# Windowed attention and a gated unit on one core: each transfer waits until few others stand in front of it in the queue, and the planner models instruction fetches

## The chip, the cores and the metric

The kernel runs on one core of one Trainium2 chip. Its five engines work side by side: PE (TensorE, matmuls and transposes), DVE (VectorE), ACT (ScalarE), POOL (GpSimd) and SP (SyncE, which here only issues transfers). Sixteen DMA engines move the data between HBM and the core's SBUF. The metric is the time of one execution on the device in microseconds; the median of three runs before the change is 193.21 us (190.97 to 197.29).

## The reference

Two stages follow each other. The first is attention over a window, for 8 batches of 8 heads with 576 positions of 64 elements; heads 0 to 3 see the last 32 positions ("plain"), heads 4 to 7 every fourth of the last 128 ("dilated"):

```python
mask_plain = (rel >= 0) & (rel < window)
mask_dil = (rel >= 0) & (rel < window * dilation) & (rel % dilation == 0)
attn = softmax(where(mask, q @ k.T / 8, -1e9))        # 8 x 8 x 576 x 576
x = (attn @ v).transpose(0, 2, 1, 3).reshape(8, 576, 512)
```

The second is a gated unit on x, a causal convolution of five taps for the gate and two dense layers:

```python
gate = sigmoid(sum(conv_w[k] * xp[:, k:k + S, :] for k in range(5)))   # xp: x, 4 zero rows ahead
out = (gate * (x @ w_val)) @ w_out                                     # 8 x 576 x 512
```

Inputs and output are float32; the kernel computes in bfloat16 with float32 sums.

## The kernel before

The attention is cut into 16 units: one for the four dilated and one for the four plain heads of each batch (`units`). The first of a batch is the dilated one, except in the last batch. Each unit is worked on in these steps:

- SP loads q and k (`load_q`, 576 KB each) and v (`load_vd` in two pieces of 320 and 448 KB, `load_vp` in two of 384 KB). There are three buffers for q and for k (`qns`, `kns`) and two for each v.
- POOL, or another engine, casts v to bfloat16, and q and k too for a plain unit (`cvq`, `cvk`, `cvv`, `cvp`).
- PE transposes q and k (`transposes`, L431); ACT and DVE copy the result out of PSUM.
- PE makes the scores in four parts (`scores`, L450), ACT takes their exponential (L470), DVE multiplies by the mask (L476), PE multiplies with v (`attn_d` L487, `attn_p` L514), and DVE divides by the sum.
- PE transposes the result (L535, L551), and ACT or DVE copies it to `xT`, where x stands with its channels on partitions.

After both units of a batch, PE runs the convolution (`conv`, L569), ACT a tanh, PE the dense layer with `w_val` (`val`, L584) and DVE the gate; then, over tiles of 128 rows, PE the layer with `w_out` (`outs`, L600), ACT copies the result to one of six tiles `osb` (L605), and SP stores it (`store`, L614). The weights are loaded in halves of 512 KB into `wst` (`load_w`) and cast. Where PE would have nothing to do at the start, it runs matmuls on a tile `warm` (L627), which nobody reads.

The order of all this is not written out. A planner in the kernel (`Plan`) lists every step as a `Task` with an estimated time on each engine that can do it, its dependences and a key; `KEY` holds an offset for each kind of step. At build time `run` goes through the tasks in the order of a modelled clock: `start_of` tells when a task could start, `commit` books it, and among those that could start soon the lowest key wins. The tasks are then emitted in the order of their modelled starts. On the chip each engine works through its own list in order and waits by semaphores for what it needs. The modelled times have no further effect.

Three parts of the planner matter here. A transfer is modelled to occupy the DMA for `load` after a fixed delay (`commit`); no more than eight transfers may be under way (`LANES`, in `start_of`); and all loads are chained in one order (`lane`). On the chip nothing but the eight semaphores of the transfers, used in turn, and the buffers hold SP back.

SP's list holds loads and stores in one order, so a store that waits for its copy holds the loads behind it.

Of the kernel before, what the change touches and what calls it, by code (L numbers as in the profile page):

```python
# [13 lines left out]
def hi_bf16(ap: bass.AP) -> bass.AP:  # L14
# [5 lines left out]
KEY = {"L": 107.8, "cv": -124.6, "T": -1.8, "ET": -73.4, "S": -44.5, "X": -131.1, "M": -134.6, "A": -61.1,  # L20
       "N": -69.6, "XT": -4.5, "XE": -25.9, "C": -13.0, "H": -17.0, "V": 4.2, "G": -107.0, "O":
       16.7, "P": -80.5, "SP": 2, "W": 23.7, "WV": 0, "WO": 1}


class Task:


    def __init__(self, name, key, opts, emit, deps=(), cfg=None, need=None,
                 frees=(), load=0.0, port=(), after=None):
        self.name, self.key, self.opts, self.emit = name, key, opts, emit  # L30
        self.deps = [d for d in deps if d is not None]
        self.cfg, self.need, self.load, self.port = cfg, need, load, port
        self.frees = [f for f in frees if f is not None]
        self.after = after
        self.holders = 0
        for f in self.frees:
            f.holders += 1
        self.fin = None
        self.slot = None


class Plan:
# [3 lines left out]
    LANES = 8  # L46
    SWITCH = 0.095
# [5 lines left out]
    def __init__(self, pairs, score_pairs):  # L53
        self.tasks = []
        self.free_at = {e: 0.0 for e in self.SLACK}
        self.banks = [0.0] * (2 * pairs)
        self.score_pairs = score_pairs
        self.scores = []
        self.cfg = None
        self.dma = 0.0  # L60
        self.lanes = []
        self.port = {"DVE": 0.0, "POOL": 0.0}
        self.idle = None
        self.done = []
# [22 lines left out]
    def start_of(self, t, eng):  # L87
        s = self.free_at[eng]
        if eng == "PE" and t.cfg != self.cfg and self.cfg is not None:
            s += self.SWITCH  # L90
        for d in t.deps:
            s = max(s, d.fin + self.LAT)
        if t.after:
            s = max(s, t.after.start)
        if eng in t.port:
            s = max(s, self.port["POOL" if eng == "DVE" else "DVE"])
        s = max(s, self.slot_for(t)[0])
        if t.load:

            while True:  # L100
                n = sum(1 for a, _ in self.lanes if a <= s)
                if n < self.LANES or self.lanes[n - self.LANES][1] <= s:
                    break
                s = self.lanes[n - self.LANES][1]
        return s
# [7 lines left out]
    def commit(self, t, eng, s):  # L113
        inf = float("inf")
        occ, lat = t.opts[eng]
        before = self.free_at[eng]
        self.free_at[eng] = s + occ
        t.fin = s + lat
        if t.load:
            self.dma = max(self.dma, s + 1.4) + t.load  # L120
            t.fin = self.dma + 0.6
            self.lanes = sorted(self.lanes + [(s, t.fin)])
        if eng in t.port:
            self.port[eng] = s + lat
        if eng == "PE":
            self.cfg = t.cfg
            self.fill(before, s)
        if t.need:
            t.slot = self.slot_for(t)[1]
            for n in t.slot:  # L130
                self.banks[n] = inf
            if t.need == "score":
                self.scores.append(inf)
                t.order = len(self.scores) - 1
            t.last = 0.0
        for f in t.frees:
            f.holders -= 1
            f.last = max(f.last, t.fin + self.LAT)
            if f.holders == 0:
                for n in f.slot:  # L140
                    self.banks[n] = f.last
                if f.need == "score":
                    self.scores[f.order] = f.last
        t.start, t.eng = s, eng
        self.done.append(t)
# [13 lines left out]
    def run(self):  # L159
        todo = list(self.tasks)  # L160
        waiting = {}
        users = {}
        ready = []
        for t in todo:
            deps = t.deps + ([t.after] if t.after else [])
            waiting[t] = len(deps)
            for d in deps:
                users.setdefault(d, []).append(t)
            if not deps:
                ready.append(t)  # L170
        inf = float("inf")
        while ready:
            best = None
            for eng in self.free_at:
                c = [(self.start_of(t, eng), t.key, t) for t in ready
                     if eng in t.opts and self.fits(t, eng)]
                c = [x for x in c if x[0] < inf]
                if not c:
                    continue
                s0 = min(x[0] for x in c)  # L180
                s, k, t = min((x for x in c if x[0] <= s0 + self.SLACK[eng]), key=lambda x: (
                    x[1] + (KEY["W"] if eng == "PE" and x[2].cfg != self.cfg else 0.0), x[0]))
                if best is None or (s, k) < best[:2]:
                    best = (s, k, t, eng)
            s, _, t, eng = best
            ready.remove(t)
            self.commit(t, eng, s)
            for n in users.get(t, []):
                waiting[n] -= 1
                if not waiting[n]:  # L190
                    ready.append(n)
        assert all(t.fin is not None for t in todo)
        for t in sorted(self.done, key=lambda t: t.start):
            t.emit(t)
# [3 lines left out]
def kernel(  # L198
# [10 lines left out]
    nc = tc.nc  # L209
# [5 lines left out]
    R = 4  # L215
# [158 lines left out]
    def dma(name, key, load, emit, deps=(), eng="SP", lane=None):  # L374
        t = plan.add(name, key, {eng: (0.45, 0.45)}, lambda t: emit(), deps, load=load,
                     after=lane and lane[0])
        if lane:
            lane[0] = t
        return t

    d_cw = dma("conv_nat", -60, 0.05,
               lambda: nc.scalar.dma_start(out=conv_nat, in_=moe_conv_w), eng="ACT")

    def load_q(u, name):
# [4 lines left out]
        if d:  # L389
            nc.sync.dma_start(  # L390
                out=dst, in_=src[b, hs].rearrange("h (p j) d -> (h p) (j d)", j=JD))
        else:
            nc.sync.dma_start(
                out=dst.rearrange("p (x f) -> p x f", x=2),
                in_=src[b, hs].rearrange("(x e) (p j) d -> (e p) x (j d)", x=2, j=JP))

    def load_vd(u, n, z):
        b = units[u][0]
        rows = v[b, 4:8].rearrange("h (p r) d -> p h (r d)", r=R)
        if z == 0:  # L400
            nc.sync.dma_start(out=vas[z][n % 2], in_=rows[0:KB[0]])
        else:
            nc.sync.dma_start(out=vas[z][n % 2][Z1:KB[1]], in_=rows[T1 + Z1:TT])

    def load_vp(u, n, half):
# [3 lines left out]
        skip = 1 if b == 0 and half == 0 else 0  # L409
        if skip:  # L410
            nc.sync.dma_start(
                out=vps[n % 2][W // 2:64, 0].rearrange("p s d -> p (s d)"),
                in_=bass.AP(tensor=v.tensor, offset=v.offset,
                            ap=[[2 * D, 64 - W // 2], [1, 2 * D]]))
        nc.sync.dma_start(
            out=dst[:, skip:].rearrange("p n s d -> p n (s d)"),
            in_=bass.AP(tensor=v.tensor, offset=first + skip * 192 * D,
                        ap=[[2 * D, 64], [192 * D, 4 * NG - skip], [1, 2 * D]]))
# [190 lines left out]
    def store(f, n, z):  # L609
        o = 0  # L610
        while o < 128:
            b, c = (128 * n + o) // HALF, (128 * n + o) % HALF
            ln = min(128 - o, HALF - c)
            nc.sync.dma_start(out=out[b, f * HALF + c:f * HALF + c + ln, :],  # L614
                              in_=osb[z % NO][o:o + ln])
            o += ln

# [24 lines left out]
    def load_w(name, src, dst, key):  # L642
        parts = []
        for half in range(2):
            deps = [W_OK["val"][2 * half], W_OK["val"][2 * half + 1]] if name == "out" else []
            ld = dma(f"w_{name}{half}", key, 1.6, lambda half=half: nc.sync.dma_start(
                out=wst[half],
                in_=src.rearrange("(c p) n -> p c n", p=128)[:, 2 * half:2 * half + 2]), deps, lane=lane)
# [38 lines left out]
    for u in range(NU):  # L687
# [4 lines left out]
        for name, L, TQ in (("q", ldq, Tq), ("k", ldk, Tk)):  # L692
# [7 lines left out]
            L[u] = dma(f"ld{name}{u}", j0 + KEY["L"], 1.75 if d else 1.85, lambda u=u, name=name: load_q(u, name), dep, lane=lane)  # L700
        if d:
            dep = [cvv[(same[-2], e, z)] for e in range(2) for z in range(2)] if len(same) > 1 else []
            ldv[u] = [dma(f"vd{z}{u}", j0 + KEY["L"], (1.25, 1.75)[z],
# [3 lines left out]
        else:  # L707
            dep = [cvp[2 * same[-2] + e] for e in range(2)] if len(same) > 1 else [c_dv]
            ldv[u] = [dma(f"vp{u}{h}", j0 + KEY["L"], 2.0,
# [18 lines left out]
        for name, L, C, TQ, EV in (("q", ldq, cvq, Tq, Eq), ("k", ldk, cvk, Tk, Ek)):  # L728
            TQ[u] = add(f"T{name}{u}", j0 + KEY["T"], {"PE": (0.50, 0.67)},
                        lambda t, u=u, name=name: transposes(t, u, name),  # L730
                        [L[u] if d else C[u], c_eye], cfg="F", need="pair")
# [4 lines left out]
        for e in range(2):  # L736
# [29 lines left out]
            for h in range(2):  # L766
# [3 lines left out]
                                 cfg="R" if d else "Q", need="score")  # L770
# [11 lines left out]
                if d:  # L782
# [3 lines left out]
                                     cfg="F", frees=[SC[(i, h)]])  # L786
# [6 lines left out]
                elif h == 1:  # L793
                    a = add(f"A{i}", j + KEY["A"], {"PE": (0.39, 0.56)},
                            lambda t, sc=SC[(i, 1)], i=i: attn_p(t, sc, i),
                            [MA[(i, 0)], MA[(i, 1)], cvp[i]], cfg="R", frees=[SC[(i, 1)]])
# [9 lines left out]
            if d:  # L806
                XT[i] = add(f"XT{i}", jx + KEY["XT"], {"PE": (0.27, 0.44)},
                            lambda t, i=i: transpose_xd(t, i),
                            [NM[(i, 0)], NM[(i, 1)]], cfg="F", need="bank")
# [3 lines left out]
            elif e == 1:  # L813
                XT[(u,)] = add(f"XT{i}", jx + KEY["XT"], {"PE": (0.52, 0.69)},
                               lambda t, u=u: transpose_xp(t, u),
                               [NM[(i, 1)], NM[(i - 1, 1)]], cfg="F", need="pair")
# [7 lines left out]
        for n, c in enumerate((2, 3, 0, 1)):  # L824
            CV[(b, c)] = add(f"C{b}{c}", j1 + KEY["C"] + n, {"PE": (0.60, 0.77)},
                             lambda t, b=b, c=c: conv(t, b, c),
                             [XE[(b, c)], T_DG], cfg="Q", need="pair")
# [3 lines left out]
        for n, c in enumerate((2, 3, 0, 1)):  # L831
# [3 lines left out]
                             cfg="F", need="pair")  # L835
# [6 lines left out]
    for n in range(NF):  # L842
        for f in range(2):
# [5 lines left out]
                     + (W_OX if f else W_OK["out"]), cfg="F", need="bank")  # L849
# [3 lines left out]
            ST.append(dma(f"st{f}{n}", key - 20, 0.8, lambda f=f, n=n, z=z: store(f, n, z), [cp]))  # L853
# [32 lines left out]
```

## Time and profile before

| what | value |
|---|---|
| median of three runs | 193.21 us |
| the profiled execution: its own time, span in the profile | 193.35 us, 191.4 us |
| PE busy; of it the filler matmuls (L627) | 166.2 us; 15.7 us |
| DVE, ACT, POOL busy | 128.4, 123.0, 61.7 us |
| moved by DMA | 43.41 MB, mean 227 GB/s |
| issue to landing, median: q, k, vp | 9.8, 11.3, 11.4 us |
| issue to landing, median: a store of 256 KB | 2.6 us |
| granted TensorE clock | 0.988 |

In the profile a line such as `L584` is a line of the kernel before. The page gives each engine's busy time, then the span in 40 slices of 4.8 us with a digit for the busy share of each, the DMA queues, the chain of work that ended last, and the groups of instructions. In the chain in order of time, a line has its start, its length and what the chain went through there; "issue" is time in which an engine waited for nothing that the profile shows. A line of waits has the waiting engine, what it waited for, the total in us, how often, and the longest. A line of DMA issues has the count, the size of each and the median time from issue to landing.

### The profile page before, as it was taken

How to read it: one execution, taken by the hardware profiler on the slowest of the kernel's cores; microseconds unless marked ns; L12 is line 12 of the kernel's file. 1: busy time of each engine (PE TensorE's matmuls, PEld its weight loads, DVE VectorE, ACT ScalarE, POOL GpSimd, SP SyncE). 2: the span in 40 equal slices, each digit the busy share in tenths (PEclk: the TensorE clock that was granted, in tenths of full speed). 3: DMA queues.
4: the chain of work that ended last, by engine and by line, in shares of the span. 5: the costliest groups of instructions: out<-in, count | busy, mean ns of one | idle time of the engine just before them, and what ended most of it. 6: DMA issues, size and time to landing. Idle time of an engine off the chain costs nothing.

```text
span 191.4 us, 6733 instructions
## 1 busy us (share of the span) xinstructions
PE 166.2 (87%) x2892; PEld 113.2 (59%) x2892; DVE 128.4 (67%) x239; ACT 123.0 (64%) x204; POOL 61.7 (32%) x99
## 2 busy tenths in 40 slices
PE   7999988788888779989896998989999989999890
PEld 2546456655676547766673765655675876757540
DVE  7498585967576858667877576997667978930500
ACT  2448976575796839768845577775786394658151
POOL 7964308236332552803632207351007000000000
PEclk9999999999999999999999699999999999999998
DMA  5999999999999999999999839996451312035256
GB/s 199 269 384 235 379 255 288 234 264 278 232 341 335 252 290 233 366 294 303 296 210 269 245 115 259 361 246 247 169 172 52 113 58 110 3 104 160 68 169 215
DMA packets 32102, 43.41 MB, mean 227 GB/s; under 512 B 1877, under 2 KB 20293, under 8 KB 32074
## 3 DMA queue, kind: packets, MB, share of 16 engines
q1 hardware_dynamic: 32064, 42.99, 81.3%
q8 instruction: 22, 0.36, 0.9%
q14 instruction: 6, 0.05, 0.1%
q10 hardware_dynamic: 10, 0.01, 0.1%
HBM read 33.56 MB, written 9.44 MB: 225 GB/s over the span
## 4 chain that ended last, share of the span: by engine, by line
PE 57%; DVE 12%; ACT 11%; DMA 9%; issue 6%; POOL 1%; ACTq 0%; SPq 0%; DVEq 0%
PE ps L600 14%; PE ps L584 13%; DMA kn<-in_k_dram 8%; PE ps L569 7%; PE ps L627 6%; PE ps L431 5%; PE ps L450 4%; ACT et L470 4%; PE ps L487 3%; ACT osb L605 3%; DVE et L476 3%; PE ps L514 2%; PE ps L535 2%; DVE qT L294 2%; ACT qT L292 2%
## 5 line engine op out<-in xcount | busy, mean ns | idle before, releaser
L470 ACT ACTIVATE et<-ps 128x576 bf16<-128x576 f32 x64 | 40.6, 653 | 17.4 <-PE ps L450 17.2
L584 PE MATMUL ps<-xT,w_val 128*128 128x288 bf16 x256 | 36.0, 286 | 3.5 <-issue 2.2
L600 PE MATMUL ps<-w_out,gy 128*128 128x512 bf16 x144 | 35.7, 380 | 2.9 <-ACT osb L605 1.9
L593 DVE SCALAR_TENSOR_TENSOR gy<-gy,ps 128x576 bf16<-128x576 bf16 x32 | 23.9, 750 | 14.9 <-PE ps L584 14.7
L605 ACT ACTIVATE osb<-ps 128x512 f32<-128x512 f32 x35 | 20.0, 598 | 18.9 <-PE ps L600 17.0
L294 POOL CAST vd<-va 80x512 bf16<-80x512 f32 (+1 forms) x32 | 20.7, 678 | 33.1 <-DMA va<-in_v_dram 14.2
L584 PEld LDWEIGHTS <-w_val 128*128 128x128 bf16 x256 | 23.7, 98 | 11.2 <-issue 5.6
L569 PE MATMUL ps<-xT,diag 64*64 64x288 bf16 x640 | 25.1, 287 | 2.4 <-issue 0.7
L294 POOL CAST vpb<-vp 128x768 bf16<-128x768 f32 x16 | 13.5, 863 | 38.6 <-DMA vp<-in_v_dram 21.7
L476 DVE TENSOR_TENSOR et<-et,mask_p 128x576 bf16<-128x576 bf16 x32 | 18.7, 591 | 7.0 <-ACT et L470 6.3
L476 DVE TENSOR_TENSOR et<-et,mask_d 128x576 bf16<-128x576 bf16 x32 | 20.2, 636 | 4.3 <-ACT et L470 3.9
L497 DVE TENSOR_TENSOR xnd<-ps,rec 72x512 bf16<-72x512 f32 x32 | 22.0, 687 | 1.1
L600 PEld LDWEIGHTS <-gy 128*128 128x128 bf16 x144 | 12.7, 98 | 15.6 <-issue 3.1
L577 ACT ACTIVATE gy<-ps 128x576 bf16<-128x576 f32 x32 | 20.2, 658 | 2.7 <-PE ps L569 2.5
L569 PEld LDWEIGHTS <-diag 64*64 64x64 bf16 x640 | 18.0, 107 | 5.3 <-issue 3.4
L292 ACT COPY xT<-ps 128x576 bf16<-128x576 bf16 (+1 forms) x20 | 15.7, 786 | 7.2 <-PE ps L551 3.7
L292 ACT COPY qT<-ps 128x576 bf16<-128x576 bf16 x22 | 13.6, 643 | 10.5 <-PE ps L431 7.8
L450 PE MATMUL ps<-qT,kT 64*64 64x96 bf16 (+1 forms) x640 | 18.6, 203 | 1.6 <-ACT kT L292 1.0
L450 PEld LDWEIGHTS <-kT 64*64 64x64 bf16 (+1 forms) x640 | 12.4, 102 | 12.3 <-issue 8.1
L627 PE MATMUL ps<-warm 128*128 128x512 bf16 x52 | 15.7, 429 | 1.3 <-DVE warm L314 1.3
L292 ACT COPY kT<-ps 128x576 bf16<-128x576 bf16 x21 | 12.9, 644 | 4.6 <-PE ps L431 2.7
L526 DVE TENSOR_TENSOR xnp<-ps,den 96x768 bf16<-96x768 f32 x16 | 15.3, 954 | 0.5
(68 smaller groups left out, 181.1 us busy)
## 6 DMA issues: line engine op xcount, KB each, us to landing
qn<-in_q_dram SPq DMA_DIRECT2D x16, 576.0 KB, 9.8
kn<-in_k_dram SPq DMA_DIRECT2D x16, 576.0 KB, 11.3
out_dram<-osb SPq DMA_DIRECT2D x24, 256.0 KB, 2.6
vp<-in_v_dram SPq DMA_DIRECT2D x15, 384.0 KB, 11.4
va<-in_v_dram SPq DMA_DIRECT2D x8, 448.0 KB, 9.9
va<-in_v_dram SPq DMA_DIRECT2D x8, 320.0 KB, 7.1
out_dram<-osb SPq DMA_DIRECT2D x8, 192.0 KB, 2.4
wst<-in_moe_w_val_dram SPq DMA_DIRECT2D x2, 512.0 KB, 8.4
```

The costliest lines, as they stand in the source:

```text
L292: nc.scalar.copy(out=dst, in_=src)
L294: op(t.eng).tensor_copy(dst, src)
L450: nc.tensor.matmul(out=ps[po:po + pn, x, out_c:out_c + ln], lhsT=kw[rb, k0:k0 + (pn - 1) * kstep + 1:kstep], rhs=qT[rb, q0:q0 + (ln - 1) * ...
L470: nc.scalar.activation(out=ets[(2 * i + hf) % NE][:, :, 0:HALF], in_=ps[:, :, 0:HALF], func=AF.Exp, scale=scale)
L476: op(t.eng).tensor_tensor(out=ev, in0=ev, in1=m.to_broadcast([128, 2, HALF]), op=ALU.mult)
L497: nc.vector.tensor_tensor(out=xnd[i % 2][:, 4 * hf:4 * hf + 4].rearrange("p (x j) h d -> p x (j h) d", x=2), in0=av[:, :, :, 0:D], in1=rec ...
L569: nc.tensor.matmul(out=ps[o:o + 64, 512 * f:512 * f + HALF], lhsT=diag[lo:lo + 64, c * K + kk, :], rhs=xT[lo:lo + 64, b % NX, c, f * HALF ...
L584: nc.tensor.matmul(out=ps[:, 512 * f:512 * f + HALF], lhsT=w_val[f][:, mc, c * 128:(c + 1) * 128], rhs=xT[:, b % NX, mc, K - 1 + f * HALF: ...
L593: nc.vector.scalar_tensor_tensor(out=y, in0=y, scalar=1.0, in1=ps[:, :, 0:HALF], op0=ALU.add, op1=ALU.mult)
L600: nc.tensor.matmul(out=ps, lhsT=y[:, c, 128 * n:128 * n + 128], rhs=w_out[f][:, c, :], start=(c == 0), stop=(c == NCH - 1))
L605: nc.scalar.activation(out=osb[z % NO], in_=bank(ou), func=AF.Copy, scale=0.5)
L627: plan.idle = lambda t: nc.tensor.matmul(out=bank(t), lhsT=warm[:, 0:128], rhs=warm, start=True, stop=True)
```

## The change

Three things change together.

Each transfer that SP issues is made to wait for an earlier one. The planner keeps the list of SP's transfers with their modelled starts (`queue`). `last_out` walks back from a transfer and adds up the `load` of those in front of it; the first at which the sum exceeds `QUEUED` (2.5 us) is the one that has to have landed. `start_of` uses it in the model, and when the kernel is emitted the same transfer is added as a dependence on the chip (`go` in `dma`). To that end the functions that load and store return their instructions.

The planner models the fetching of PE's program: tasks carry their number of matmuls (`mm`); after every `LINE` (125) matmuls a fetch of `FETCH` (1.3 us) is booked on the modelled DMA, and PE cannot pass into a block before its fetch is over.

The constants of the model and all of `KEY` are new: `load` is 1.5 us for q and k instead of 1.75 and 1.85, 1.2 and 1.6 or 1.72 for v, 1.36 for a weight half, 0.68 for a store; the fixed delays of a transfer are 0.9 and 0.1 us instead of 1.4 and 0.6. `WV` and `WO` move the loads of `w_val` behind unit 1 and of `w_out` behind unit 2; they stood behind units 0 and 1. No step of the computation is added or taken away. The order on every engine is another one, and the fillers on PE are 40 instead of 52.

```diff
-KEY = {"L": 107.8, "cv": -124.6, "T": -1.8, "ET": -73.4, "S": -44.5, "X": -131.1, "M": -134.6, "A": -61.1,
-       "N": -69.6, "XT": -4.5, "XE": -25.9, "C": -13.0, "H": -17.0, "V": 4.2, "G": -107.0, "O":
-       16.7, "P": -80.5, "SP": 2, "W": 23.7, "WV": 0, "WO": 1}
+KEY = {"L": 119.7, "cv": -131.4, "T": -6.8, "ET": -106.9, "S": -24.3, "X": -162.2, "M": -79.5, "A": -90.6,
+       "N": -64.4, "XT": -0.9, "XE": -52.1, "C": -4.6, "H": -36.9, "V": -0.2, "G": -170.8, "O":
+       14.2, "P": -84.3, "SP": 2, "W": 5.4, "WV": 1, "WO": 2}
...
+    LINE = 125
+    FETCH = 1.3
+    QUEUED = 2.5
...
+        if eng == "PE":
+            s = max(s, self.lines.get((self.mm + t.mm) // self.LINE, 0.0))
...
-        if t.load:
-
+        if t.load and eng == "SP":
             while True:
-                n = sum(1 for a, _ in self.lanes if a <= s)
-                if n < self.LANES or self.lanes[n - self.LANES][1] <= s:
+                d = self.last_out(s, len(self.queue))
+                n = sum(1 for d in self.queue if d.start <= s)
+                if n >= self.LANES:
+                    e = self.queue[n - self.LANES]
+                    if d is None or e.fin > d.fin:
+                        d = e
+                if d is None or d.fin + self.LAT <= s:
                     break
-                s = self.lanes[n - self.LANES][1]
+                s = d.fin + self.LAT
         return s
+
+    def last_out(self, s, n):
+
+        ahead = 0.0
+        for d in reversed(self.queue[:n]):
+            if d.start <= s:
+                ahead += d.load
+                if ahead > self.QUEUED:
+                    return d
+        return None
...
         if t.load:
-            self.dma = max(self.dma, s + 1.4) + t.load
-            t.fin = self.dma + 0.6
-            self.lanes = sorted(self.lanes + [(s, t.fin)])
+            self.dma = max(self.dma, s + 0.9) + t.load
+            t.fin = self.dma + 0.1
+            if eng == "SP":
+                t.start = s
+                self.queue = sorted(self.queue + [t], key=lambda d: d.start)
...
         if eng == "PE":
+            n = self.mm // self.LINE
+            self.mm += t.mm
+            for n in range(n + 1, self.mm // self.LINE + 1):
+                self.dma = max(self.dma, s + 0.5) + self.FETCH
+                self.lines[n + 1] = self.dma + 0.3
...
+        for n, t in enumerate(self.queue):
+            t.behind = self.last_out(t.start, n)
         for t in sorted(self.done, key=lambda t: t.start):
             t.emit(t)
...
     def dma(name, key, load, emit, deps=(), eng="SP", lane=None):
-        t = plan.add(name, key, {eng: (0.45, 0.45)}, lambda t: emit(), deps, load=load,
+        def go(t):
+            t.ins = emit()
+            if getattr(t, "behind", None):
+                tc.add_manual_dep(t.ins[0].ins, t.behind.ins[-1].ins.name, mybir.DependencyInfo(
+                    mybir.DependencyClass.Sync, mybir.DependencyReason.DATA),
+                    reason="few transfers in the queues")
+
+        t = plan.add(name, key, {eng: (0.45, 0.45)}, go, deps, load=load,
                      after=lane and lane[0])
...
-            L[u] = dma(f"ld{name}{u}", j0 + KEY["L"], 1.75 if d else 1.85, lambda u=u, name=name: load_q(u, name), dep, lane=lane)
+            L[u] = dma(f"ld{name}{u}", j0 + KEY["L"], 1.5, lambda u=u, name=name: load_q(u, name), dep, lane=lane)
...
-            ST.append(dma(f"st{f}{n}", key - 20, 0.8, lambda f=f, n=n, z=z: store(f, n, z), [cp]))
+            ST.append(dma(f"st{f}{n}", key - 20, 0.68, lambda f=f, n=n, z=z: store(f, n, z), [cp]))
```

## The prediction

> **What bounds the kernel now.** I read the page first: engines, slices, queues, chain. No engine is full; PE leads with 166 us, of which 15.7 us are filler matmuls on the tile `warm`. The slices show a DMA that is full for 110 us and slack after that, and the queue rows show a second stream beside the data:
>
> ```profile
> PE 166.2 (87%) x2892; PEld 113.2 (59%) x2892; DVE 128.4 (67%) x239; ACT 123.0 (64%) x204; POOL 61.7 (32%) x99
> ...
> DMA  5999999999999999999999839996451312035256
> ...
> q1 hardware_dynamic: 32064, 42.99, 81.3%
> q8 instruction: 22, 0.36, 0.9%
> ...
> PE 57%; DVE 12%; ACT 11%; DMA 9%; issue 6%; POOL 1%; ACTq 0%; SPq 0%; DVEq 0%
> ...
> kn<-in_k_dram SPq DMA_DIRECT2D x16, 576.0 KB, 11.3
> out_dram<-osb SPq DMA_DIRECT2D x24, 256.0 KB, 2.6
> ```
>
> A load lands 11.3 us after its issue, though transfers of its size follow each other by about 1.45 us: the rest is queue. Queue q8 carries PE's own program: 22 blocks of 16 KB, 256 instructions each.
>
> Then the chain of waits in order of time:
>
> ```profile
> 20.06 15.26 DMA kn<-in_k_dram
> 35.37 1.16 POOL kc L294
> ...
> 44.30 0.79 issue
> ...
> 52.29 0.66 PE ps L431 x9
> ...
> 53.14 0.34 issue
> ...
> 59.52 0.70 issue
> ...
> 65.41 0.37 PE ps L584 x3
> 65.78 2.23 issue
> 68.01 0.80 PE ps L584 x5
> ...
> 103.68 0.87 issue
> ```
>
> Two things are to be seen. Up to 52.3 us arrivals set the pace: unit 5's keys land at 50.5, are cast on POOL, and PE transposes them at 52.29; after that no load is on the chain. And PE stops in the middle of a group (three of eight matmuls of one `val`, then 2.23 us of nothing). Counting PE's records in the trace, these stops stand exactly 256 apart: 44.3, 53.1, 59.5, 65.8, 81.1, 95.3, 103.7 us, for 0.79, 0.34, 0.70, 2.23, 0.91, 0.88 and 0.86 us, 6.7 us in all. Each ends 1.3 to 1.6 us after a q8 packet has ended. They are instruction fetches that came late. A q8 packet begins 2.4 to 6.0 us after the crossing before it while five to seven transfers are in flight, 1.7 and 2.4 us after it with two, and 0.2 to 0.9 us with none or one (after 110 us, where no stop is left). So the wait depends on the queued transfers.
>
> **What the Trainium skill says.** *Runtime: NRT & Kernel Launch*, section Instruction fetch mechanics: programs come in blocks of 16 KiB or 256 instructions, fetched ahead, and crossing a block is "mostly hidden". The block size agrees; seven of 22 crossings here are not hidden. *DMA: Bandwidth & Descriptors*, section Queues, rings and completion order: a DMA engine alternates between queues packet by packet. Then a fetch would pass queued data quickly; the 2.4 to 6.0 us speak against that here. The same page, Anatomy of one DMA: waits are held on the issuing sequencer, not in the DMA engines. So every added wait holds SP and all that is queued behind it. And its section on why a DMA increments its semaphore by 16: a transfer has landed when the last of its parts has. In this trace the sixteenth update follows the first by 0.8 us at the start, by up to 4.3 us at 103 us, and by 0.2 us for a lone store.
>
> **Part by part.** *Fewer transfers in front.* The built order shows load i waiting, nearly everywhere, for load i-2 to land, so about two are in flight instead of five to seven. A fetch then waits some 2 us, takes 1.0 to 1.5 us, and PE may go on 1.4 us later: about 4.7 us. I priced PE's groups by slots read from the chain (T 0.57 us for nine transposes, scores 0.2 for eight and 0.3 for twelve, attention 0.27 and 0.47, transposes of x 0.27 and 0.6, conv 0.74, val 1.0, out 0.9). In the new order one block of 256 instructions, among the first where PE waits for loads anyway, holds 4.3 us of work, the others 5.3 and more, so all seven stops should go. Those after 52.3 us count: 5.9 us. The first, 0.79 us, is covered by the load wait at 52.3. Bounds: -5.9 and -3.
>
> *The throttle while loads are the bound.* The first load's issue to first packet takes 1.04 us; its predecessor in flight carries 1.45 us of data, so the queue should not run dry. I take 0.7 us over the 26 transfers that are needed before 52.3 us; bounds 0 and 5 (0.2 us each). A gain is excluded: the same bytes come in the same order up to that point, except that `w_val` moves behind unit 1 and `w_out` behind unit 2. That brings unit 1's v earlier by about the two 1.36 us pieces of `w_val`, but units 3 to 5 not, and 40 fillers instead of 52 only fill a wait.
>
> *The new order on PE.* Total work is equal, 149 us by my slots (32 transposes of q or k 18.2, 64 scores 16, attention 8.6 and 7.5, 24 transposes of x 9.1, 32 conv 23.7, 32 val 32, 36 out 32.4, small ones 1.4); the dependences are counted in the same slots. Up to the transposes of unit 5's keys it is 30.4 us before and 29.3 after, so 1.1 us more remains: +1.1. Beyond the fetch stops PE loses 9.9 us after 52.3 (186.64 - 52.29 - 118.6 of work - 5.9). In the new order the dependent groups stand somewhat further apart: from the key transposes to their scores the smallest distance is 0.3 us of PE work against 0.0, the tenth percentile 1.7 against 1.4; from `val` to `out` the tenth percentile is 7.2 against 5.0; from attention to the transposes of x the median is 5.9 against 3.0. I take -1.2 us, bounds -4 and +2.
>
> *Loads behind stores.* In the SP order stores now come earlier among the loads, and a store waits for ACT's copy; SP has 67 us of such waits already:
>
> ```profile
> SPq L614 <- ACT osb L605: 67.5, 24, 6.5
> ...
> POOL kc L294 <- DMA kn<-in_k_dram: 11.4, 7, 2.2
> ```
>
> From the `out` group whose store stands last before a load to the first use of that load there were 15 to 36 us of PE work; there are now 8 to 25, most 9 to 15. The way is: copy 0.6 us plus up to 1 us in ACT's queue, two store issues and one load issue at 0.4, landing some 2.5 us later, 1.5 for one transfer ahead, and a cast of 1.15 us on POOL: about 8 us, or 9.3 with a fetch of 1.3. Five places have less than 9.5. I take +1.0 us, bounds 0 and +10. Waits in front of the last stores cost nothing: there they land in about 2.5 us as before.
>
> *Retuned keys and planner constants* emit nothing but this order; one answer with the above.
>
> Sum: -5.9 + 0.7 + 1.1 - 1.2 + 1.0 = -4.3 us. The profiled execution took 193.35 us (span 191.4, 1.95 us around it), which is at the median of the runs shown, 193.21. Forecast: 189.0 us, a span of 187.1.
>
> **The rivals.**
> *Everything helps* (0.14): the earlier unit 1 also lets PE build a lead, and latency gaps shrink by their bound of 4: 189.0 - 3.5 = 185.5 us. For: 12 fillers fewer. Against: the same arrivals for units 3 to 5.
> *No net gain* (0.24): either two in flight leave the queue dry for 0.2 us at each of 26 transfers, 189.0 + 4.3 = 193.3 us; or fetches do not get faster, because they wait their turn some other way, and the change doesn't do what it says: 189.0 + 5.9 = 194.9 us. For: the first three transfers are slow (landings at 4.73, 6.12, 8.29 us). Against: the fetches after 110 us.
> *Slower* (0.20): loads issued just in time. A late copy on ACT (its longest wait for an `out` is 3.6 us) holds a store, which holds the loads behind it; they land 1.5 to 2 us after their use at some six places of the middle, 10 us: 199 us. It decides once the way from `out` to cast exceeds the 8 to 10 us of PE work in between; before, 15 and more covered it. For: SP's 67.5 us behind ACT. Against: those waits lie mostly after the loads.
> *Forecast* (0.42): 189.0, its own range 186.5 to 191.5.
>
> **How the numbers follow.** About 2% (3.9 us) is what a measurement of this kernel tells from no change; its three runs alone span 191 to 197. Faster means under 189.35: the first rival and some two thirds of the forecast, 0.42. Slower means over 197.1: most of the last rival, 0.18. The rest, 0.40, is within. The range goes from just under the first rival, 185.0, to 198.0, which leaves out about one half of the slower case and a little at the low end.
>
> **What would show it.** In the new profile: no "issue" stop over 0.3 us at every 256th PE record; loads landing 3 to 5 us after their issue instead of 10 to 11; transposes of unit 5's keys near 53 us; no load on the chain after that. Wrong would be: DMA entries on the chain between 60 and 150 us, POOL's waits for loads (49.5 us now: vp 21.7, va 14.2, kn 11.4, qn 2.2) grown well beyond 50, or unit 5's keys later than 55 us.

## The result and the profile after

The changed kernel takes 209.53 us (208.30 to 211.41), the kernel before in the same comparison 193.33 us: a ratio of 1.089, with an interval of 1.074 to 1.105. It is slower by 9%, or 16 us, and lies outside the predicted range. Some executions of a kernel are slower by 1.5% or more than its fastest; a ratio here compares only the others, so it is not always the quotient of the medians beside it. The profiled execution of the changed kernel took 208.3 us, with a span of 206.5; its mean granted clock was 0.961, against 0.988.

These are the lines of the changed kernel's page that answer to those shown of the kernel before:

```profile
PE 167.3 (81%) x2880; PEld 114.9 (56%) x2880; DVE 124.0 (60%) x236; ACT 124.2 (60%) x208; POOL 59.6 (29%) x98
...
DMA  6778778758788658577877978849877886153065
...
q1 hardware_dynamic: 32064, 42.99, 69.4%
q8 instruction: 22, 0.36, 0.8%
...
DMA 45%; PE 27%; ACT 9%; issue 6%; DVE 5%; POOL 3%; SPq 1%; ACTq 1%; POOLq 0%; DVEq 0%
...
kn<-in_k_dram SPq DMA_DIRECT2D x16, 576.0 KB, 4.8
out_dram<-osb SPq DMA_DIRECT2D x24, 256.0 KB, 3.0
```

PE does the same work (167 us). The DMA row is what changed. It stood at 9 from the second slice to 110 us; now it stands mostly at 5 to 8 up to 165 us, with two slices at 9, so the same bytes take longer, and the DMA is seldom full. Transfers have become the largest part of the chain, 45% instead of 9%. A load of k lands 4.8 us after its issue instead of 11.3: the queue in front of it is gone, as intended.

The chain in order of time shows how the loads follow each other (start, length, what):

```profile
4.84 3.13 DMA va<-in_v_dram
7.98 4.81 DMA qn<-in_q_dram
13.20 4.07 DMA vp<-in_v_dram
17.29 4.47 DMA wst<-in_moe_w_val_dram
21.77 5.00 DMA qn<-in_q_dram
...
57.54 4.88 DMA kn<-in_k_dram
62.54 1.64 POOL kc L324
64.22 1.14 PE ps L468 x9
...
79.87 6.71 DMA kn<-in_k_dram
87.50 4.88 DMA qn<-in_q_dram
92.40 4.49 DMA va<-in_v_dram
96.95 4.41 DMA qn<-in_q_dram
```

Each of the first lines begins where one before it ends: the transfer issued at 4.84 us has landed at 7.97, and 7.98 is the next start. A transfer is issued only when the one two places ahead of it has landed, and needs 4 to 5 us itself. The issue and landing times of the trace say the same: the first k of unit 0 is issued at 1.27 us, with one transfer in front; the two pieces of v wait for the landings of q (4.82) and k (6.21) and are issued at 4.84 and 6.23; the next q and k wait for those pieces (7.97, 10.14) and are issued at 7.98 and 10.16. Unit 5's keys, which landed at 50.54 us before, land at 62.41. Up to there the chain is mostly load after load, and after 79 us it is on loads again.

The waits of POOL, which casts what arrives, and of SP (engine and line, what it waited for, total in us, times, longest):

```profile
POOL vd L324 <- DMA va<-in_v_dram: 46.2, 12, 9.3
POOL vpb L324 <- DMA vp<-in_v_dram: 31.8, 7, 7.7
POOL kc L324 <- DMA kn<-in_k_dram: 16.6, 7, 5.6
POOL qc L324 <- DMA qn<-in_q_dram: 11.3, 6, 5.9
```

```profile
SPq L651 <- ACT osb L642: 20.3, 11, 5.4
SPq L427 <- DMA vp<-in_v_dram: 18.0, 11, 3.1
SPq L429 <- DMA va<-in_v_dram: 16.7, 10, 3.3
SPq L438 <- DMA kn<-in_k_dram: 15.3, 7, 4.0
```

POOL waits 105.9 us for loads instead of 49.5. SP's waits for ACT's copies, 67.5 us before, have shrunk to 20.3; in their place it waits for landings. SP is not held by stores; it is held by the added wait itself.

PE's stops at every 256th of its records are gone: 6.8 us in all before (the prediction's seven, and one of 0.09 us), 0.12 us now, and that is a wait for DVE. A fetch now mostly begins 0.2 to 2.7 us after the crossing instead of 2.4 to 6.0.

### The profile page after: what moved, and what is told of

Its sections match the earlier page's. It is cut to its first block, busy times and chain, and to the rows that moved or that the text cites. A ratio compares the mean times of both kernels' runs of the same rounds, so it can differ in the third digit from the quotient of the medians.

```text
span 206.5 us, 6700 instructions
## 1 busy us (share of the span) xinstructions
PE 167.3 (81%) x2880; PEld 114.9 (56%) x2880; DVE 124.0 (60%) x236; ACT 124.2 (60%) x208; POOL 59.6 (29%) x98
## 4 chain that ended last, share of the span: by engine, by line
DMA 45%; PE 27%; ACT 9%; issue 6%; DVE 5%; POOL 3%; SPq 1%; ACTq 1%; POOLq 0%; DVEq 0%
DMA qn<-in_q_dram 13%; DMA kn<-in_k_dram 13%; PE ps L637 8%; DMA va<-in_v_dram 6%; PE ps L621 6%; DMA vp<-in_v_dram 6%; PE ps L606 4%; PE ps L468 4%; ACT osb L642 3%; DMA wst<-in_moe_w_out_dram 2%; ACT kT L322 2%; DMA wst<-in_moe_w_val_dram 2%; ACT et L507 2%; DVE et L513 2%; POOL kc L324 2%
## 5 line engine op out<-in xcount | busy, mean ns | idle before, releaser
L507 ACT ACTIVATE et<-ps 128x576 bf16<-128x576 f32 x64 | 39.7, 653 | 10.6 <-PE ps L487 10.4
L324 POOL CAST vd<-va 80x512 bf16<-80x512 f32 (+1 forms) x32 | 19.5, 637 | 51.0 <-DMA va<-in_v_dram 46.2
L642 ACT ACTIVATE osb<-ps 128x512 f32<-128x512 f32 x36 | 20.5, 600 | 14.7 <-PE ps L637 8.7
L606 PE MATMUL ps<-xT,diag 64*64 64x288 bf16 x640 | 25.7, 295 | 1.8 <-ACT xT L322 1.6
L322 ACT COPY qT<-ps 128x576 bf16<-128x576 bf16 x24 | 14.6, 642 | 17.0 <-PE ps L468 11.5
L324 POOL CAST vpb<-vp 128x768 bf16<-128x768 f32 x16 | 13.3, 860 | 36.0 <-DMA vp<-in_v_dram 31.8
L322 ACT COPY kT<-ps 128x576 bf16<-128x576 bf16 x24 | 14.6, 642 | 14.1 <-PE ps L468 8.2
L513 DVE TENSOR_TENSOR et<-et,mask_d 128x576 bf16<-128x576 bf16 x32 | 17.8, 563 | 7.5 <-ACT et L507 6.9
L513 DVE TENSOR_TENSOR et<-et,mask_p 128x576 bf16<-128x576 bf16 x32 | 17.7, 575 | 6.5 <-ACT et L507 6.2
L487 PEld LDWEIGHTS <-kT 64*64 64x64 bf16 (+1 forms) x640 | 12.7, 106 | 11.9 <-issue 8.5
L524 PE MATMUL ps<-vd,et 80*128 80x65 bf16 (+1 forms) x256 | 14.1, 200 | 6.0 <-DVE et L513 2.8
L524 PEld LDWEIGHTS <-et 80*128 80x128 bf16 (+1 forms) x256 | 11.3, 101 | 11.3 <-DVE et L513 8.1
```

Source lines behind the costliest of these rows:

```text
L322: nc.scalar.copy(out=dst, in_=src)
L324: op(t.eng).tensor_copy(dst, src)
L487: nc.tensor.matmul(out=ps[po:po + pn, x, out_c:out_c + ln], lhsT=kw[rb, k0:k0 + (pn - 1) * kstep + 1:kstep], rhs=qT[rb, q0:q0 + (ln - 1) * ...
L507: nc.scalar.activation(out=ets[(2 * i + hf) % NE][:, :, 0:HALF], in_=ps[:, :, 0:HALF], func=AF.Exp, scale=scale)
L513: op(t.eng).tensor_tensor(out=ev, in0=ev, in1=m.to_broadcast([128, 2, HALF]), op=ALU.mult)
L524: nc.tensor.matmul(out=ps[:, x * 512 + c * DA:x * 512 + (c + 1) * DA], lhsT=et[0:KB[z], x, c * QB:c * QB + 128], rhs=vds[z][n][:, hh, 2 * ...
```

## The experiments

The change has two parts that can be set apart: the wait on the chip, and the new order on all engines (keys, constants, modelled fetches). In what follows "old order" and "new order" are those of the two kernels; each experiment keeps one of them on every engine exactly, unless it says otherwise. "Fetch stops" is the sum of PE's stops at its 256-record crossings, and "keys" is when unit 5's keys land, both from the profiled execution. A stop at a crossing can also be a wait for another engine that happens to fall there; where the trace shows one, it is said. The theory that came out of the traces is that two transfers in flight cannot keep the DMA engines busy. Its rivals are that the new order is at fault, and that loads stand behind stores that wait for ACT.

### The two parts, one at a time

The new order without the wait:

```diff
         for n, t in enumerate(self.queue):
-            t.behind = self.last_out(t.start, n)
+            t.behind = None
```

> The order of every engine as in the changed kernel, with the added wait of each transfer taken away; the eight semaphores alone hold transfers back. Theory 1, two transfers in flight starve the DMA: unit 5's keys land near 51 us instead of 62.4, the fetch stops at every 256th PE record come back (some 5 us), and the time falls to 190 to 197 us. Theory 2, the new order is at fault (loads behind stores, weights later): the time stays at 204 us or more.

Measured: 193.66 us, ratio 1.0004 (0.9951 to 1.0058). Keys at 49.08 us, fetch stops 2.05 us, of which 0.73 us were a wait for ACT's copy; fewer came back than the 5 us expected. So the new order by itself is neither faster nor slower than the old one, and the whole loss of the changed kernel comes with the wait: 1.089 against 1.000. But this order has some 5 us less of fetch stops than the old one and does not gain by them, so something else in it should cost about as much.

The old order with the wait: `last_out` and `go` are added to the kernel before, with the changed kernel's loads (1.5 us for q and k, and so on) in the sum, and nothing else of the change.

```diff
+    QUEUED = 2.5
+    REAL = {1.75: 1.5, 1.85: 1.5, 1.25: 1.2, 2.0: 1.72, 1.6: 1.36, 0.8: 0.68}
...
+        for n, t in enumerate(self.queue):
+            t.behind = self.last_out(t.start, n)
```

> The order of every engine as in the kernel before, with the added wait alone (2.5 us of transfers in front, counted with the new loads). Theory 1: unit 5's keys land near 62 us, no fetch stops, 203 to 210 us. Theory 2: at or below the kernel before, 187 to 194 us.

Measured: 215.05 us, ratio 1.1124 (1.1029 to 1.1219), keys at 60.92 us, and no fetch stop: the one stop of 0.54 us at a crossing is a wait for POOL's cast. The time is longer than the 203 to 210 us expected. The wait costs 21 us in the old order and 16 in the new one, which was planned for it. That the new order is the culprit is refuted: with this wait it is the better of the two.

### How many transfers have to be in flight

A kernel that leaves out all computation (its output is zeros) issues loads of 576 KB from SP, twelve with one in flight, then twelve each with two, three, four and eight, held back by the same kind of wait; then stores of 256 KB.

```diff
+    for depth in (1, 2, 3, 4, 8):
+        made = []
+        for i in range(12):
+            d = load(n)
+            n += 1
+            if i >= depth:
+                after(d, made[i - depth])      # wait until that one has landed
...
+            made.append(d)
```

> All computation is left out: only 60 loads of q and k of 576 KB, twelve each with at most 1, 2, 3, 4 and 8 in flight, then 36 stores of 256 KB, twelve each with 1, 2 and 8. Theory 1: from landing to landing 4.0 us with one, about 2.2 with two, 1.6 to 1.8 with three, 1.45 with four and eight; stores 2.1, 1.1 and 0.7 us. What I had assumed in the prediction: 1.45 to 1.5 us from two on.

The stretches with 1, 2, 3, 4 and 8 loads in flight (from:to, length, busy of DVE and POOL, clock, DMA share, GB/s):

```profile
0.00:44.00 44.00, 0.48 (x1) 0.20 (x4) 1.00 0.48 161
47.50:71.00 23.50, 0.00 (x0) 0.00 (x0) 1.00 0.75 259
74.80:93.20 18.40, 0.00 (x0) 0.00 (x0) 1.00 0.90 333
97.40:113.20 15.80, 0.00 (x0) 0.00 (x0) 1.00 0.96 378
117.30:133.20 15.90, 0.00 (x0) 0.00 (x0) 1.00 0.93 375
```

| in flight | landing to landing, us | issue to landing once so many are in flight, us |
|---|---|---|
| 1 | 3.6 | 3.3 to 3.75 |
| 2 | 2.14 | 3.4 to 5.3 (median 4.6) |
| 3 | 1.69 | 4.5 to 5.5 |
| 4 | 1.44 | 5.6 to 5.9 |
| 8 | 1.45 | 10.9 to 11.8 |

This is one execution, but with the runs above and the other depths below it settles the cause. Four loads in flight fill the DMA engines, and more only lengthen the queue. With two in flight a load takes 2.14 us where it could take 1.44. The changed kernel's figures are those of the second row: 4.8 us from issue to landing, a DMA share of 0.72 to 0.82 in the stretches up to 62.5 us, and 212 to 228 GB/s there (its pieces of v are smaller than these loads; the kernel before moves 255 to 335 GB/s in the same stretches).

The lone load shows why. Of its 3.6 us about 1.0 passes before the first packet, about 2.3 until the last packet ends, and some 0.3 until the last of the sixteen parts has reported. The Trainium skill, *DMA: Bandwidth & Descriptors*, Anatomy of one DMA, gives a fixed 2.0 us and bytes over 436 GB/s for transfers issued from GpSimd; for 576 KB that is an estimate of 3.35 us, and the measured 3.6 from SP is near it. The planner of the changed kernel books 0.9 + 1.5 + 0.1 = 2.5 us for the same load.

### The wait at other depths

In the old order, `QUEUED` at 4.0, 5.5 and 7.0 us, that is about three, four and five loads in flight:

```diff
-    QUEUED = 2.5
+    QUEUED = 5.5
```

> The order of the kernel before with the added wait alone at 5.5 us, about four in flight. Theory 1: unit 5's keys land at 50 to 52 us as before, and of the 6.8 us of fetch stops under 2 are left: 187 to 191 us, faster than before. If the fetch stops were covered by other waits, no change: 192 to 195 us.

> The same at 4.0 us, about three in flight: 1.7 us per load instead of 1.44 puts unit 5's keys at 53 to 56 us, fetch stops under 1 us; 191 to 198 us, by theory 1 above the run with 5.5 us.

> The order of the kernel before with about four transfers in flight, timed more closely beside 7.0 us. 185 to 189 us; 3 to 4% under the kernel before.

> The same at 7.0 us, about five in flight. A fifth adds nothing to a DMA that four fill, and some 1.5 us to each fetch: 188 to 192 us, with 2 to 5 us of fetch stops. If the fetch stops don't matter, equal to the run with 5.5 us.

| old order, wait | in flight | keys, us | fetch stops, us | median, us | ratio to before (interval) |
|---|---|---|---|---|---|
| 2.5 | 2 | 60.92 | 0 | 215.05 | 1.1124 (1.1029 to 1.1219) |
| 4.0 | 3 | 51.77 | 0 | 190.27 | 0.9881 (0.9809 to 0.9953) |
| 5.5 | 4 | 48.25 | up to 0.5 | 187.54 | 0.9648 (0.9533 to 0.9764) |
| 5.5, again | 4 | 50.28 | 0 | 187.07 | 0.9679 (0.9600 to 0.9758) |
| 7.0 | 5 | 52.55 | 3.81 | 191.99 | 0.9866 (0.9810 to 0.9922) |
| none (the kernel before) | 5 to 7 | 50.54 | 6.8 | 193.3 to 194.0 | 1 |

(In the first run at 5.5 PE stops for 1.63 us at one crossing, 102.4 us; for all but 0.5 us of it, it also waits for POOL's cast.) The fetch stops grow with the number of transfers in flight, and the wait alone was changed, so late fetches do come from the queued transfers. The loads are far behind only with two in flight. In between lies a best place: with four in flight the loads come as early as without a wait, and nearly all fetch stops are gone. Three in flight did better than expected (191 to 198 us, keys at 53 to 56). The page of that kernel (the first run at 5.5):

```profile
PE 163.0 (89%) x2892; PEld 111.7 (61%) x2892; DVE 126.4 (69%) x239; ACT 122.2 (67%) x204; POOL 61.4 (34%) x99
...
DMA  5999999999999999999999999999863013044166
...
q1 hardware_dynamic: 32064, 42.99, 84.4%
...
PE 48%; ACT 17%; DMA 15%; DVE 13%; issue 4%; POOL 0%; SPq 0%; ACTq 0%; DVEq 0%; POOLq 0%
...
kn<-in_k_dram SPq DMA_DIRECT2D x16, 576.0 KB, 7.2
```

The DMA row is full again, with a landing in 7.2 us instead of 11.3 or 4.8. This kernel is faster than both others: 187.07 us, 3.2% under the kernel before.

### The new order at other depths

The plan stays that of the changed kernel; only the wait on the chip is longer:

```diff
+    ON_CHIP = 4.0                      # and 5.5
...
-            t.behind = self.last_out(t.start, n)
+            t.behind = self.last_out(t.start, n, self.ON_CHIP)
```

> The changed kernel's order; the wait on the chip counts up to 4.0 us in front instead of 2.5, so about three transfers are in flight. Theory 1: most of the loss goes, unit 5's keys land at 53 to 55 us, 193 to 199 us. Theory 2: no change from the changed kernel, 204 us or more.

> The changed kernel's order; the wait on the chip counts up to 5.5 us in front, so about four transfers are in flight. Theory 1, about four in flight fill the DMA and more only lengthen the queue: unit 5's keys land at 49 to 52 us, fetch stops stay under 1.5 us in all, 188 to 193 us. Were a still shorter queue the gain, it would be slower than with 4.0 us (192.1 us) by 3 us or more, as the fetch stops come back.

Measured: at 4.0, 192.09 us, ratio 0.9888 (0.9843 to 0.9932), keys at 51.85 us, and no fetch stop (the one of 0.12 us is a wait for DVE); both are better than expected. At 5.5, 191.51 us (188.19 to 192.24) beside 193.97 for the kernel before, too few runs for an interval; keys at 48.46 us, fetch stops 1.63, of which 1.29 us are a wait for ACT's copy. One transfer more in flight takes 17 us off the changed kernel, and the keys are 10.6 us earlier: the step from two to three is what the change lost by.

The value 4.0 in the plan too, so that the planner orders everything anew for it:

```diff
-    QUEUED = 2.5
+    QUEUED = 4.0
```

> The changed kernel with 4.0 us instead of 2.5 both in the planner's model and on the chip; keys and all else as there, so the order on the engines is planned anew. Theory 1: like the run with 4.0 us on the chip alone, 189 to 196 us. If the order planned for the short queue mattered most, it would differ from that run by more than 5 us.

Measured: 194.42 us, ratio 1.0062 (1.0020 to 1.0104), keys at 53.51 us, and no fetch stop (the one of 0.45 us is a wait for DVE). This planning for the depth did not help; this order is a little worse than the two others at the same wait.

### Are loads behind stores what is left?

With the two orders at 5.5 us stands 191.5 against 187.5 us, though the keys agree and fetch stops are nearly gone in both. SP waits for ACT's copies 68.2 us in the new order there, and 37.3 us in the old. In the new order without a wait SP waits for ACT's copies longer than in any other kernel here:

```profile
SPq L651 <- ACT osb L642: 97.8, 26, 18.4
```

The longest, 18.4 us, holds the loads behind it, and the DMA stands nearly idle from 49 to 56 us. To test whether that is the difference, ACT issues the stores instead of SP, at 5.5 us and in both orders; the wait then counts loads alone:

```diff
-            ins.append(nc.sync.dma_start(out=out[b, f * HALF + c:f * HALF + c + ln, :],
+            ins.append(nc.scalar.dma_start(out=out[b, f * HALF + c:f * HALF + c + ln, :],
...
+        self.queue = [t for t in self.queue if not t.name.startswith("st")]
```

> The changed kernel's order at 5.5 us, but the stores are issued by ACT right after its copy instead of by SP, so that no load stands behind a store on SP; ACT pays some 0.4 us for each of 48 issues. If loads behind stores are why the new order is 4 us slower than the old at 5.5 us: 186 to 189 us, and the idle DMA near 50 us is gone. If the rest of the order is why: 191 us or more.

> The same move of the stores in the old order, where loads stand far ahead of the stores: no gain, and ACT's issues cost up to 4 us: 187 to 192 us.

Measured: 206.46 us, ratio 1.0814 (1.0730 to 1.0897), in the new order, and 201.99 us, ratio 1.0449 (1.0357 to 1.0541), in the old one. Both lose about 15 us, far more than I allowed for, and the difference between the orders is still there, 4.5 us. So loads held behind stores are not shown to be what the new order loses by; the test is a weak one, because the edit costs so much itself. Much of where it goes can be seen in the chain, and in ACT's waits, of the old order with stores on ACT:

```profile
72.73 7.47 DMA kn<-in_k_dram
...
80.22 0.36 ACTq L644
```

```profile
ACT kT L315 <- DMA kn<-in_k_dram: 4.4, 1, 4.4
ACT xT L315 <- DMA qn<-in_q_dram: 3.3, 1, 3.3
```

L644 is the issue of a store, now on ACT. It begins at 80.22 us, when a load of keys that SP issued at 72.73 has landed; the trace has it waiting for the semaphore that this load raises (loads and stores share eight of them). By then ACT has stood idle for 4.4 us, and what comes behind the store on ACT has to wait. The same happens at 53.8 us behind a load of q. Each of these two waits in the list ends with such an issue; with the stores on SP, ACT has no wait for q or k in this order. The loads themselves are not what is late: up to 106 us they land within about 2 us of where they land with the stores on SP (the same keys at 80.2 against 78.4 us), while in the stretch from 62.5 to 90 us PE is busy for 21.5 us against 25.9. In the new order ACT is held once for 5.0 us in the same way. How much of the 15 us this makes in all was not set apart from the 48 issues themselves and a lower clock.

## Why the prediction was wrong

*What bounds the kernel; fetches.* Right. The stops at every 256th record went, 6.8 to 0.12 us (that one a wait for DVE), and a gain of the size of their -5.9 us is to be had: the old order with four in flight, which changes nothing but the wait, gains 3.2% (interval 2.4 to 4.0), or 6.2 us, with the stops down to 0 to 0.5. Not all of that need be the stops: the keys land 0.3 to 2.3 us earlier, and the granted clock is higher (0.990 against 0.980), which by the estimate in the last section goes with 1.7 us. The rival by which fetches would not get faster falls.

*"The throttle while loads are the bound", +0.7 us with bounds of 0 and 5.* This is the step that failed. Measured at unit 5's keys it is +11.9 us against the kernel before (62.41 - 50.54), 0.46 us for each of the 26 transfers, and +13.3 against the same order without the wait (62.41 - 49.08). The argument was that "its predecessor in flight carries 1.45 us of data, so the queue should not run dry". 1.45 us is what a load takes in a full queue; it is no lone load's duration. Two things were overlooked. The next transfer is released not by the end of the data but by the landing, the last of sixteen reports. And the two in flight have shared the DMA engines, so that when the first lands part of the second's data has gone already (in the depth run with two in flight 4 to 107 of its 128 packets, 46 on average), and less than 1.45 us is left to cover 1.04 us until the next first packet. The trace of before held what was needed: a first load landing about 4 us after its issue, when nothing stood in front of it. Divided by the 1.45 us of the full queue that asks for almost three in flight at the least; the depth run needed four.

*The rival "no net gain"* named this mechanism, the queue running dry, and gave it 0.2 us each. The mechanism was right and the size was off by more than two: 0.46 us. With that size the forecast would have been 189.0 - 0.7 + 11.9 = 200.2 us, on the slow side, and still 9.3 us short of the measured 209.5.

*After the keys.* Between their landing and the end of the profiled span lie 140.9 us before and 144.1 in the changed kernel. How much of it the wait costs in the new order is known only roughly. The trace of that order without the wait has 146.1 us, but its execution, 196.9 us, was 3.2 us longer than that kernel's median. By the medians the wait costs 15.9 us (209.5 - 193.7), so beside the 13.3 at the keys some 2.6 us come after them. In the old order the same wait makes this part 154.0 us. Against the kernel before, this part is 3.2 us longer although 5.9 us of fetch stops have gone from it, so 9.1 us came in elsewhere: with the keys' 11.9 and the -5.9 that is the 15.1 us by which the span has grown. The 9.1 us were not split between the new order, the loads on the chain and the lower clock.

*The new order: +1.1 - 1.2 + 1.0 = +0.9 us.* Without the wait the order is as fast as before while its fetch stops are some 5 us fewer, so it should cost about 5 us elsewhere. So of the 20.5 us by which the forecast missed, 15.9 come with the wait and 4.6 (193.7 - 189.0) are there without it. The 5 us are inside the bounds of the three terms and larger than their sum. Against the old order it stands at about 4 us worse with four in flight, at no difference in the ratios with three (0.9888 against 0.9881; 192.1 and 190.3 us as medians), and 5.5 us better with two. It was planned for late loads and is better only where they are late. Which of its distances between dependent groups costs the time is open; none was tried alone.

*The rival "slower", by loads just in time behind stores,* ends on the right side for another reason: SP's waits for copies fell from 67.5 to 20.3 us in the changed kernel. All three signs that were to show the forecast wrong are there: transfers on the chain between 60 and 150 us, POOL's load waits at 105.9 us, keys later than 55 us. Two that were to show single steps right, no stops and landings after 3 to 5 us, are there as well. Short latency had been read as a gain; it was the sign of a queue too short to be full.

## What to carry to other kernels

A wait that limits the transfers in flight has a floor: the time from issue to landing of one transfer alone, divided by the spacing of such transfers in a full queue, rounded up and one more; here 3.6 / 1.44 gives three, and four was measured. The one more comes from this case alone, and three already beat the kernel before. Below the floor every transfer that is needed costs its share of the latency, and above it the queue only lengthens what waits behind it, instruction fetches too. Take the lone duration from a transfer that had nothing in front of it, and try one part of such a change on the old order first: the wait alone, set to four, was worth more than all the planning around it.

## What the runs showed beside this

- Loads of 576 KB reach 161, 259, 333, 378 and 375 GB/s with 1, 2, 3, 4 and 8 in flight, all from one queue. A store of 256 KB takes 2.05 us alone, 0.99 each with two in flight and 0.68 with eight.
- PE's instruction fetches come the later the more transfers are queued for data: 6.8, 3.8, 0 to 0.5 and 0 us of stops in the old order with 5 to 7, 5, 4 and 3 in flight. By which way they wait for each other was not seen.
- Stores issued from ACT instead of SP, 48 of them, came with 14.5 to 15 us more. A store's issue on ACT was held until a load issued by SP had landed, with ACT idle for up to 5.0 us at a time and its work behind the issue late.
- The kernels held to two in flight were granted a lower TensorE clock: 0.960 on average in the changed kernel and 0.919 in the old order, against 0.980 over 40 runs of the kernel before. Over the 90 runs of the kernel before that were timed beside the experiments, a clock lower by 0.01 goes with about 1.6 us more (a straight line through widely scattered points). An estimate by this line puts about 3 of the changed kernel's 16 us down to the clock, and 10 of the 21 us in the old order, where the line is drawn far beyond its points. What is cause and what effect was not tested, and nothing was taken out of the times above.
